# Sharing transposes two tiles at a time from tile 2 on, a later first output product, and a modulation vector folded by DMA, in an adaLN block with linear attention and a token mixer

## The chip, the cores and the metric

The kernel runs on one core of a Trainium2 chip. A core has TensorE (matrix products, "PE" in the profile), VectorE (DVE), ScalarE (ACT), GpSimd (POOL) and SyncE (SP, which here only issues transfers). The metric is the time of one execution on the device in microseconds, less being better; a kernel's time is the median of its runs.

## The reference

One token sequence x of 2048 x 448 goes through an attention half and a token-mixing MLP half. Both are modulated by six vectors of 448 that come from one condition vector c:

```python
mod = (silu(c) @ w_mod).reshape(1, 6, 1, -1)
sa, ca, ga, sb, cb, gb = (mod[:, j] for j in range(6))
h = layernorm(x) * (1 + ca) + sa
x = x + ga * A(h)          # linear attention
h = layernorm(x) * (1 + cb) + sb
x = x + gb * B(h)          # token-mixing MLP

# A: 16 heads of 28; phi(t) = where(t > 0, t + 1, exp(t)) + 1e-6
q, k, v = split(h @ wqkv)
kv = einsum("bhsd,bhse->bhde", phi(k), v);  z = sum over s of phi(k)
o = (phi(q) @ kv) / (phi(q) . z + 1e-6)
A = o @ wo
# B: the MLP runs over the token axis, F = 1792
u = gelu(einsum("bsd,sf->bdf", h, w1) + b1)
B = transpose(einsum("bdf,fs->bds", u, w2) + b2)
```

All data are float32.

## The kernel before

The 2048 tokens lie in 16 tiles of 128 rows by 448 channels (NT = 16). A float32 product is made of three TensorE products of a reduced float32 type: each operand is cut into a high part (a rounding copy, on ScalarE) and a low part (the difference, on VectorE), and high x high, high x low and low x high are added up in one PSUM bank. Channels are taken in chunks of 128; the fourth chunk has only 64 channels, and the other 64 rows of it can hold something else, such as low parts. That is how a product of 448 channels takes eleven matmuls instead of twelve: the 64 remaining channels of the high part and of the low part lie in one 128-row operand.

The order in which each engine works is written out by hand, in the order of the code; each engine works through its own list, and a step waits only for the data and the buffers that it needs. So what stands ahead of a step on its engine delays it, also where the two have nothing to do with each other.

The change lies in one stage, the loop `for i in range(NT + LAG)` with LAG = 5, from about 115 to 226 us. It runs the output side of the attention, the second layer norm, and the first GEMM of the MLP as a pipeline over tiles, and TensorE does in iteration i:

- the transposes of tile i (`b_transpose`, bank `tq`): the normalised q of the tile, `pn`, is turned chunk by chunk so that channels lie on partitions;
- output product i-1 (`b_out`, bank `op`): the transposed tile, in parts `pth` and `ptl`, times weights that hold wo with the attention state folded in. These weights are computed ahead of the loop in four groups of 112 rows (four heads each), in parts `wph` and `wpl`, and are moved by transfers into chunks of 128 rows, `oh` (high) and `ol` (low). Tile 0 uses the groups of 112, in twelve matmuls; the others use the chunks, in eleven;
- some q products of later tiles (`a_q`, bank `qp`, eleven matmuls each), as `QS` says: one an iteration, and two in iterations 0 and 4;
- from iteration 5 on, the step of w1's GEMM for tile i-5 (`step`, banks `up`).

VectorE and ScalarE do for the same tiles: the cut into `pth` and `ptl` (`b_high`, `b_low`); the residual `x` with its row sum (`b_res`, tile i-2); the second layer norm with its modulation in pieces (`b_norm1_a`, `b_norm1_b` on tile i-3, `b_norm2` on tile i-4), whose squares `sqa` (of x) and `sqb` (of y) are made on ScalarE and whose inverse roots `rt` and bias `nb` are made on GpSimd; the parts `h2h` and `h2l` of the result; and the normalisation of q for a tile ahead, s (`b_prod`, `b_sum`, `b_eps`, `b_recip`, `b_scale`: names `pd`, `den`, `pn`). `s` is i + 1, and i + 2 behind iteration LEAD = 4, in which two tiles are normalised. Between these, pieces of w1 are cut into `ph` and `pl` (`split_to`): the high and low part on ScalarE (L283, L284), and a transfer on GpSimd that adds (L285).

From tile B_PAIR = 6 on, tiles go in pairs: the fourth transpose of the first tile of a pair holds the last 64 channels of both tiles, the second tile has only three transposes, and two small transfers on SyncE (L850) bring the low parts where the product needs them. For tiles ahead of the pairs, VectorE copies the last 64 channels of `pn` next to themselves (`b_dup`), and each tile has four transposes.

Modulation vector 5 (gb) is also made in this stage. `w_mod`'s block lies as four tiles `wm` of 112 rows; `mod_part(5, k)` adds up the four, each scaled by its part of silu(c), in `acc` (the first on ScalarE, the others on VectorE). `mod_split` cuts `acc` into `mh` and `ml`, and `mod_sum2(5)`, at the start of iteration 16 and ahead of its `up` matmuls, adds their 112 rows with a matrix of ones into bank `modp`. For the vectors 2, 3 and 4 (`FOLDED`) rows 64 to 111 of `acc` are first added to rows 0 to 47 by an accumulating transfer on GpSimd (`fold`, L197), so that high and low part, 64 rows each, make one operand `mb` and one matmul:

```python
    def fold(j):
        nc.gpsimd.dma_start(macc[j][:G - 64], macc[j][64:], accum_op=ALU.add)

    def mod_split(j):
        acc = macc.pop(j)
        if j in FOLDED:
            macc[j] = moving(slot, f"mb{j}")
            split(acc[:64], macc[j][:64], macc[j][64:])
            return
```

(G is 112.) In the orders shown below, a number behind a name is the tile's, and the one behind the underscore the buffer's.

## Time and profile before

| | |
|---|---|
| median of 3 runs | 437.97 us (437.65 to 438.12) |
| the profiled execution | 438.2 us, of which the span from the first to the last instruction is 436.4 us |
| TensorE busy | 431.4 us (99% of the span) |
| VectorE busy | 365.6 us (84%) |
| ScalarE busy | 270.8 us (62%) |
| GpSimd busy | 122.1 us (28%) |
| granted TensorE clock | 1.000 |

"Busy" is the time in which an engine has an instruction in work; matmuls overlap in TensorE's pipeline, so the distance between the starts of two of them, and not the duration of one, is what one costs. In the profile's rows stand the start in us, the duration in us, the engine, the line of the kernel, the operation, the operands as out<-in, and in square brackets the idle time ahead of it and what ended that. The chain that ended last is followed back from the last instruction: at each step to what released it, or to the instruction before it on its engine.

### The profile page before, as it was taken

How to read it: one execution, taken by the hardware profiler on the slowest of the kernel's cores; microseconds unless marked ns; L12 is line 12 of the kernel's file. 1: busy time of each engine (PE TensorE's matmuls, PEld its weight loads, DVE VectorE, ACT ScalarE, POOL GpSimd, SP SyncE). 2: the span in 40 equal slices, each digit the busy share in tenths (PEclk: the TensorE clock that was granted, in tenths of full speed). 3: DMA queues.
4: the chain of work that ended last, by engine and by line, in shares of the span. 5: the costliest groups of instructions: out<-in, count | busy, mean ns of one | idle time of the engine just before them, and what ended most of it. 6: DMA issues, size and time to landing. Idle time of an engine off the chain costs nothing.

```text
span 436.4 us, 7337 instructions
## 1 busy us (share of the span) xinstructions
PE 431.4 (99%) x2390; PEld 401.8 (92%) x2390; DVE 365.6 (84%) x791; ACT 270.8 (62%) x581; POOL 122.1 (28%) x201
## 2 busy tenths in 40 slices
PE   8999999999999999999999999999999999999997
PEld 7699999999999999999999999999999999999996
DVE  5997898999899999985479487349999998898894
ACT  3768877765758787776766254235675555655650
POOL 2205767431034665554300000010112230230310
PEclk9999999999999999999999999999999999999999
DMA  8987999994442232524427456477667977977531
GB/s 223 307 220 117 175 206 237 223 226 140 139 124 50 39 65 58 145 66 90 127 84 237 166 161 183 125 183 196 153 141 188 187 161 181 183 162 202 88 43 44
DMA packets 66558, 65.97 MB, mean 151 GB/s; under 512 B 8776, under 2 KB 58072, under 8 KB 66520
## 3 DMA queue, kind: packets, MB, share of 16 engines
q1 hardware_dynamic: 55728, 48.41, 37.7%
q0 software_dynamic: 10784, 17.09, 24.9%
q8 instruction: 19, 0.31, 0.3%
q14 instruction: 19, 0.16, 0.1%
q10 hardware_dynamic: 8, 0.00, 0.0%
HBM read 41.88 MB, written 7.34 MB: 113 GB/s over the span
## 4 chain that ended last, share of the span: by engine, by line
PE 97%; DMA 1%; DVE 1%; SPq 0%; issue 0%; DVEq 0%
PE y L1129 19%; PE up L914 10%; PE up L916 10%; PE up L915 10%; PE y L1130 9%; PE op L864 8%; PE cacc L483 8%; PE qp L384 8%; PE kp L384 7%; PE tp L353 2%; PE tq L829 1%; DMA wm<-in_w_mod_dram 1%; PE kvb L757 1%; PE kp L532 1%; PE qp L532 1%; PE wp L934 1%
## 5 line engine op out<-in xcount | busy, mean ns | idle before, releaser
L914 PE MATMUL up<-h2h,ph 128*128 128x448 f32 x224 | 81.4, 363 | 0.0
L916 PE MATMUL up<-h2h,pl 128*128 128x448 f32 x224 | 81.3, 363 | 0.0
L915 PE MATMUL up<-h2l,ph 128*128 128x448 f32 x224 | 80.8, 361 | 0.0
L1089 POOL DMA_DIRECT2D a<-a x16 | 14.1, 969 | 147.2 <-PE up L915 75.6
L916 PEld LDWEIGHTS up<-h2h,pl 128*128 128x128 f32 x224 | 42.0, 188 | 3.2
L915 PEld LDWEIGHTS up<-h2l,ph 128*128 128x128 f32 x224 | 42.0, 187 | 2.8
L914 PEld LDWEIGHTS up<-h2h,ph 128*128 128x128 f32 x224 | 42.0, 188 | 2.4
L85 DVE TENSOR_TENSOR pl<-pr,ph 128x512 fp32r<-128x512 f32 x38 | 25.9, 689 | 11.4 <-ACT ph L84 8.8
L84 ACT ACTIVATE ph<-pr 128x512 fp32r<-128x512 f32 x38 | 23.2, 621 | 17.8 <-PE up L915 7.3
L1151 ACT ACTIVATE cc<-y 128x448 f32<-128x448 f32 x24 | 13.0, 544 | 22.8 <-PE y L1130 22.8
L483 PE MATMUL cacc<-pkh,xh 128*128 128x448 f32 x64 | 24.3, 379 | 0.0
L483 PE MATMUL cacc<-pkl,xh 128*128 128x448 f32 x64 | 23.2, 362 | 0.0
L1172 POOL DMA_DIRECT2D out_dram<-yt x14 | 13.2, 939 | 32.5 <-DVE yt L1158 23.0
L384 PE MATMUL qp<-wh,hh 128*128 128x448 f32 x60 | 21.6, 365 | 0.0
L384 PE MATMUL qp<-wh,hl 128*128 128x448 f32 x60 | 21.5, 363 | 0.0
L905 ACT ACTIVATE y<-y,nb,rt 128x448 f32<-128x448 f32 x16 | 12.2, 762 | 13.8 <-POOL nb L904 13.8
L384 PE MATMUL kp<-wh,hl 128*128 128x448 f32 x56 | 20.4, 364 | 0.0
L384 PE MATMUL kp<-wh,hh 128*128 128x448 f32 x56 | 20.3, 362 | 0.0
L330 POOL TENSOR_TENSOR rs<-ve,mhalf 128x1 f32<-128x1 f32 x16 | 13.7, 857 | 21.6 <-DVE ve L328 20.6
L864 PE MATMUL op<-oh,pth 128*128 128x448 f32 x50 | 19.4, 387 | 0.0
L1095 DVE TENSOR_TENSOR a<-a,s 128x512 f32<-128x512 f32 (+1 forms) x32 | 18.5, 621 | 0.0
L1129 PE MATMUL y<-ut,s1h 128*128 128x448 f32 x56 | 18.2, 376 | 0.0
(253 smaller groups left out, 1373.9 us busy)
## 6 DMA issues: line engine op xcount, KB each, us to landing
pr<-in_B_w_dram SPq DMA_DIRECT2D x56, 256.0 KB, 3.0
a<-in_B_w_dram SPq DMA_DIRECT2D x32, 256.0 KB, 4.2
a<-in_B_w_dram SPq DMA_DIRECT2D x32, 192.0 KB, 4.7
wm<-in_w_mod_dram SPq DMA_DIRECT2D x24, 196.0 KB, 4.8
x<-in_A_x_dram SPq DMA_DIRECT2D x16, 224.0 KB, 3.7
out_dram<-x SPq DMA_DIRECT2D x14, 224.0 KB, 2.0
out_dram<-yt POOLq DMA_DIRECT2D x14, 224.0 KB, 4.9
pk<-pk POOLq DMA_DIRECT2D x12, 224.0 KB, 4.3
```

What stands on the lines that cost most here:

```text
L84: nc.scalar.activation(hi, full, AF.Copy)
L85: nc.vector.tensor_sub(lo, full, hi.bitcast(F32))
L384: nc.tensor.matmul(o, a[:, ch * P:(ch + 1) * P], b, start=(n == 0), stop=(n == 10))
L483: nc.tensor.matmul(cacc[ch][:, :D], a[:, s], b, start=(t == 0 and i == 0), stop=(t == NT - 1 and i == len(todo) - 1))
L864: nc.tensor.matmul(opb[t][:, :D], a[:, g * P:(g + 1) * P], b, start=(n == 0), stop=(n == len(todo) - 1))
L914: nc.tensor.matmul(ps[:, :D], hi[:, sl], mh, start=first, stop=False)
L915: nc.tensor.matmul(ps[:, :D], hi[:, sl], ml, start=False, stop=False)
L916: nc.tensor.matmul(ps[:, :D], lo[:, sl], mh, start=False, stop=last)
L1089: nc.gpsimd.dma_start(w, a, accum_op=ALU.add)
L1095: nc.vector.tensor_tensor(w, raw2[q, a][i], raw2[q, b][i], op=op)
L1129: nc.tensor.matmul(ps[:, :D], h[:, s], w, start=opens and r == r0, stop=False, skip_group_check=True)
L1130: nc.tensor.matmul(ps[:, :HD], l[:, s], wh, start=False, stop=closes and r == PAIRS - 1 - (LAST if (q, m) == (NP - 1, 6) else 0), skip_gro ...
```

## The change

Four things, in the same loop:

- Pairs begin with tile 2 instead of 6 (`B_PAIR`), so (2,3) and (4,5) also share a fourth transpose. `LEAD` becomes 1: two tiles of q are normalised in iteration 1 instead of 4. The extra q product of iteration 4 moves to iteration 1 (`QS`).
- In iteration 1 the two q products come ahead of output product 0, which stands behind four q products altogether. It now uses the 128-row chunks `oh` and `ol`, in eleven matmuls, and so tile 0 is transposed with 128 columns a time and its last 64 channels are copied, like any other tile's.
- Vector 5 is folded like 2, 3 and 4: one `modp` matmul instead of two.
- The sums of vector 5 move: they were at the starts of iterations 13, 14 and 15 and at the end of 15; now two are at the end of iteration 13, two at the end of 14, with the fold behind them, and the split stays at the end of 15.

```diff
--- before.py
+++ after.py
@@ -34,12 +34,12 @@
 LAST = 3
 PRE2 = {16: (1, 0), 12: (1, 1), 8: (1, 2), 3: (4, 3), 1: (4, 4)}
 MOD_AT = {11: [(4, 0)], 12: [(4, 1)], 13: [(4, 2)], 14: [(4, 3)], 15: [(3, 0), (3, 1)]}
-QS = {0: 2, 4: 2}
-B_PAIR = 6
-LEAD = 4
+QS = {0: 2, 1: 2}
+B_PAIR = 2
+LEAD = 1
 REM = 3 * P
 SPLIT_AT = (8, 8, 9, 10, 11, 12, 12, 13, 13, 14, 14, 15, 15, 16, 17, 18)
-FOLDED = (2, 3, 4)
+FOLDED = (2, 3, 4, 5)
 WARM = 9
 ACT_STATS = ()
 PRE = 9
@@ -773,6 +773,7 @@
     b_prod(1)
     b_recip(0)
     b_scale(0)
+    nc.vector.tensor_copy(pns[0][:, D:], pns[0][:, REM:D])
     mod_out(4, mp)
     a_phi_q()
     b_sum(1)
@@ -822,14 +823,14 @@
     def b_transpose(t):
         pn = pns[t]
         tps[t] = bank(f"tq{t}")
-        n = P if t else G
+        n = P
         pair, second = b_pair(t)
         for g in range(3 if second else 4):
             a = pns[t + 1] if pair and g == 3 else pn
             nc.tensor.transpose(tps[t][:n, g * P:(g + 1) * P], a[:, g * n:(g + 1) * n], ident)
 
     def b_high(t):
-        n = P if t else G
+        n = P
         pair, second = b_pair(t)
         if not second:
             phs[t] = (slot(f"pth{t}", 512, F32R, parts=n), slot(f"ptl{t}", 512, F32R, parts=n))
@@ -840,7 +841,7 @@
             nc.scalar.activation(phs[t + 1][0][:64, REM:], tps[t][:64, REM:], AF.Copy)
 
     def b_low(t):
-        n = P if t else G
+        n = P
         pair, second = b_pair(t)
         w = REM if second else 4 * P
         hi, lo = phs[t]
@@ -854,9 +855,7 @@
         opb[t] = bank(f"op{t}")
         todo = []
         for g in range(4):
-            if t == 0:
-                todo += [(ph, g, Wph[g]), (ph, g, Wpl[g]), (pl, g, Wph[g])]
-            elif g == 3 and b_pair(t)[0]:
+            if g == 3 and b_pair(t)[0]:
                 todo += [(ph, g, Wr[0]), (ph, g, Wr[64])]
             else:
                 todo += [(ph, g, Wp_hi[g]), (pl, g, Wp_hi[g])] + ([(ph, g, Wp_lo[g])] if g < 3 else [])
@@ -947,15 +946,17 @@
     for i in range(NT + LAG):
         if i == NT - 4:
             load_mod(5)
-        if NT - 3 <= i < NT:
-            mod_part(5, i - NT + 3)
         if i < NT:
             b_transpose(i)
+        nq = min(len(late), QS.get(i, 1))
+        if i == 1:
+            for _ in range(nq):
+                a_q(late.pop(0))
         if 0 <= i - 1 < NT:
             b_out(i - 1)
-        nq = min(len(late), QS.get(i, 1))
-        for _ in range(nq):
-            a_q(late.pop(0))
+        if i != 1:
+            for _ in range(nq):
+                a_q(late.pop(0))
         t = i - LAG
         mp = mod_sum2(5) if i == NT else None
         if t >= 0:
@@ -1003,18 +1004,25 @@
             b_low2(i - 4)
         if i == LEAD:
             wp_rest()
-            for f in (b_prod, b_sum, b_eps, b_recip, b_scale, b_dup):
+            for f in (b_prod, b_sum, b_eps):
                 f(s + 1)
         while lagging:
             phi_q_sum(lagging.pop(0))
+        if i == LEAD:
+            for f in (b_recip, b_scale, b_dup):
+                f(s + 1)
         a_phi_q(nq, lagging)
         if i == 0:
             split_low(8)
         load_to(14 + (i + 1) // 2)
         if res or norm1:
             b_rstd(i, 0 if res else 1, 2 if norm1 else 1)
+        if i in (NT - 3, NT - 2):
+            for k in (0, 1):
+                mod_part(5, 2 * (i - NT + 3) + k)
+        if i == NT - 2:
+            fold(5)
         if i == NT - 1:
-            mod_part(5, 3)
             mod_split(5)
         split_to(SPLIT_AT[i] if i < NT else 10 + (i + 1) // 2)
 
```

Lines behind the first inserted one (L776 of the changed kernel) are numbered one higher than before up to the output product, and one lower from there on: the residual is L872 for L873, the second normalisation's y is L904 for L905, `nb` L903 for L904.

VectorE, from the low part of tile 1's transposes to the residual of tile 0 and what follows it, before:

```order
224 L847 TENSOR_TENSOR ptl1_1713<-tq1_1682,pth1_1712 128x512
225 L700 RECIPROCAL den2_1717<-den2_1717 128x16
226 L704 SCALAR_TENSOR_TENSOR pn2_1722<-pq2_866,den2_1717 128x448
227 L820 COPY pn2_1722<-pn2_1722 128x64
228 L408 SCALAR_TENSOR_TENSOR pq7_1725<-eq7_1676,rq7_1677 128x448
229 L873 SCALAR_TENSOR_TENSOR x0_91,sm0_1767<-op0_1687,x0_91 128x448
230 L690 SCALAR_TENSOR_TENSOR pd3_1769<-pq3_526,zb_1538 128x448
231 L694 TENSOR_REDUCE den3_1776<-pd3_1769 128x16
232 L847 TENSOR_TENSOR ptl2_1765<-tq2_1735,pth2_1764 128x512
```

and in the changed kernel:

```order
225 L848 TENSOR_TENSOR ptl1_1725<-tq1_1683,pth1_1724 128x512
226 L700 RECIPROCAL den2_1729<-den2_1729 128x16
227 L704 SCALAR_TENSOR_TENSOR pn2_1734<-pq2_866,den2_1729 128x448
228 L690 SCALAR_TENSOR_TENSOR pd3_1742<-pq3_526,zb_1538 128x448
229 L694 TENSOR_REDUCE den3_1744<-pd3_1742 128x16
230 L408 SCALAR_TENSOR_TENSOR pq7_1747<-eq7_1677,rq7_1678 128x448
231 L700 RECIPROCAL den3_1744<-den3_1744 128x16
232 L704 SCALAR_TENSOR_TENSOR pn3_1750<-pq3_526,den3_1744 128x448
233 L821 COPY pn3_1750<-pn2_1734 128x64
234 L872 SCALAR_TENSOR_TENSOR x0_91,sm0_1796<-op0_1712,x0_91 128x448
235 L690 SCALAR_TENSOR_TENSOR pd4_1798<-pq4_620,zb_1538 128x448
236 L694 TENSOR_REDUCE den4_1805<-pd4_1798 128x16
```

The whole normalisation of tile 3 (pd, den, reciprocal, pn) now stands ahead of the residual x0, and behind x0 comes tile 4's instead of tile 3's; the copy for the shared transpose takes tile 2's channels into tile 3's buffer.

ScalarE, around the end of iteration 13, before:

```order
266 L313 ACTIVATE sqb9_2589,vs12_2574<-y9_2577,ny9_2587 128x448
267 L184 ACTIVATE acc5_2599<-wm5_0_2519,sc_158 112x448
268 L837 ACTIVATE pth13_2559<-tq13_2601 128x384
269 L905 ACTIVATE y9_2577<-y9_2577,nb9_2634,rt12_2597 128x448
270 L908 ACTIVATE h2h9_2637<-y9_2577 128x448
271 L313 ACTIVATE sqa11_2643,vs13_2642<-x11_863,nm11_2640 128x448
272 L313 ACTIVATE sqb10_2655,vs13_2642<-y10_2645,ny10_2653 128x448
273 L283 ACTIVATE ph15_2668<-pr15_1531 128x512
274 L284 ACTIVATE pl15_2669<-ph15_2668 128x512
275 L837 ACTIVATE pth14_2703<-tq14_2674 128x512
```

and in the changed kernel:

```order
270 L904 ACTIVATE y9_2579<-y9_2579,nb9_2634,rt12_2599 128x448
271 L907 ACTIVATE h2h9_2637<-y9_2579 128x448
272 L313 ACTIVATE sqa11_2643,vs13_2642<-x11_863,nm11_2640 128x448
273 L313 ACTIVATE sqb10_2655,vs13_2642<-y10_2645,ny10_2653 128x448
274 L184 ACTIVATE acc5_2668<-wm5_0_2521,sc_158 112x448
275 L283 ACTIVATE ph15_2671<-pr15_1531 128x512
276 L284 ACTIVATE pl15_2672<-ph15_2671 128x512
277 L838 ACTIVATE pth14_2705<-tq14_2676 128x512
```

The first sum of vector 5 (L184) stood ahead of the high part of tile 13's transposes; it now stands one iteration later, between the squares and the two pieces of w1.

GpSimd, end of iteration 14, in the changed kernel:

```order
150 L896 TENSOR_SCALAR vw14_2736<-vs14_2721 128x2
151 L898 TENSOR_TENSOR rt14_2738<-vw14_2736,mhalf_87 128x2
152 L197 DMA acc5_2668<-acc5_2668 48x448
153 L285 DMA pl16_2744<-pr16_1533 128x512
154 L903 TENSOR_TENSOR nb11_2779<-ny11_2731,rt14_2738 128x1
```

Before, the piece's transfer (L285) stood right behind `rt14`; now the fold (L197) stands between them, ahead of `nb11`, for which ScalarE's y11 waits.

## The prediction

> **What bounds the kernel now.** I read the page first (busy shares, clock, chain), then the waits of TensorE, then the chain and the timelines of the stage that changes.
>
> ```profile
> span 436.4 us, 7337 instructions
> ...
> PE 431.4 (99%) x2390; PEld 401.8 (92%) x2390; DVE 365.6 (84%) x791; ACT 270.8 (62%) x581; POOL 122.1 (28%) x201
> ...
> PEclk9999999999999999999999999999999999999999
> ...
> PE 97%; DMA 1%; DVE 1%; SPq 0%; issue 0%; DVEq 0%
> ```
>
> TensorE is busy for 431.4 of 436.4 us, the chain that ended last runs 97% over it, and its granted clock never drops. The list of TensorE's waits has two entries, the larger of them:
>
> ```profile
> PE warm L148 <- DVE mhalf L102: 1.1, 1, 1.1
> ```
>
> Both lie in the first microseconds. So in the changed stage (about 115 to 226 us) TensorE never waits: each matmul that goes saves its pitch, as long as nothing new makes TensorE wait. The question is therefore whether the operands still come in time. The chain in that stage:
>
> ```profile
> 120.55 0.44 PE tq L829 x4
> 120.99 2.40 PE op L864 x12
> ...
> 126.05 2.21 PE op L864 x11
> ...
> 194.65 0.33 PE tq L829 x3
> ```
>
> A 448-wide matmul takes 2.21/11 = 0.20 us of the chain, a transpose 0.44/4 = 0.11 us. The end of the stage that matters is modulation vector 5, on TensorE's timeline:
>
> ```profile
> 201.63 0.37 PE L214 MATMUL modp<-mh,ones_r 112*128 112x448 f32 x1
> 201.83 0.37 PE L215 MATMUL modp<-ml,ones_r 112*128 112x448 f32 x1
> 202.04 0.37 PE L914 MATMUL up<-h2h,ph 128*128 128x448 f32 x1
> ```
>
> **What is saved on TensorE.** Output product 0: twelve matmuls become eleven, 2.40 − 2.21 = 0.19 us, taken as 0.20. Pairs (2,3) and (4,5) share their fourth transpose: two transposes of 0.11, 0.22 us. Vector 5: two matmuls become one, 0.20 us. Sum 0.62 us, 0.14% of the time. The first tile's transposes write 128 rows instead of 112: same count, nothing. This is all that the change can gain. By 201.63 the first two items are in, so the matmul of vector 5 is reached at 201.63 − 0.42 = 201.21 if nothing waits.
>
> **What is moved early.** Output product 0 goes behind two more q products (22 matmuls, 4.4 us): it is issued at 120.99 + 4.42 = 125.41. It now needs the folded weights oh and ol, which the second output product at 126.05 already used without a wait; 0.64 us earlier I take as free, the bound being 0.64 if they came just then. The residual x0 of tile 0 is then later, and so is everything behind it on VectorE, in order:
>
> ```profile
> 124.39 0.62 DVE L873 SCALAR_TENSOR_TENSOR x<-op,x 128x448 f32<-128x448 f32 x1
> ...
> 124.93 0.62 DVE L690 SCALAR_TENSOR_TENSOR pd<-pq,zb 128x448 f32<-128x448 f32 x1
> 125.59 0.62 DVE L694 TENSOR_REDUCE den<-pd 128x16 f32<-128x448 f32 x1
> ...
> 127.33 0.24 DVE L700 RECIPROCAL den<-den 128x16 f32<-128x16 f32 x1
> 127.60 0.62 DVE L704 SCALAR_TENSOR_TENSOR pn<-pq,den 128x448 f32<-128x448 f32 x1
> ...
> 131.65 0.68 DVE L887 SCALAR_TENSOR_TENSOR y<-y,rt,mod 128x448 f32<-128x448 f32 x1
> ```
>
> Before, x0 stood at 124.39 and the second half of its normalisation, y0, at 131.65. Now op0 ends at 127.62, so x0 starts at 127.67. Between x0 and y0, VectorE also does a whole extra tile of q normalisation (pd, den, reciprocal, pn: by the starts above 0.6 + 0.6 + 0.3 + 0.6, some 2 us), since tile s+1 is prepared in iteration 1 instead of 4 and every later iteration is one tile ahead. Walking VectorE's new order with these durations gives y0 at 134.1, 2.46 us later. What waits for y0 is the loop between ScalarE and GpSimd that makes the second normalisation:
>
> ```profile
> 137.39 0.76 ACT L905 ACTIVATE y<-y,nb,rt 128x448 f32<-128x448 f32 x1 [1.00 <-POOL nb L904]
> ...
> 186.41 0.76 ACT L905 ACTIVATE y<-y,nb,rt 128x448 f32<-128x448 f32 x1 [0.90 <-POOL nb L904]
> ...
> 187.69 0.66 ACT L313 ACTIVATE sqa<-x,nm 128x448 f32<-128x448 f32 x1
> ...
> 188.35 0.66 ACT L313 ACTIVATE sqb<-y,ny 128x448 f32<-128x448 f32 x1
> ...
> 189.00 0.62 ACT L283 ACTIVATE ph<-pr 128x512 fp32r<-128x512 f32 x1
> 189.65 0.64 ACT L284 ACTIVATE pl<-ph 128x512 fp32r<-128x512 f32 x1
> ...
> 190.67 0.25 ACT L840 ACTIVATE pth<-tq 64x128 fp32r<-64x128 f32 x1
> ...
> 191.90 0.76 ACT L905 ACTIVATE y<-y,nb,rt 128x448 f32<-128x448 f32 x1 [0.98 <-POOL nb L904]
> ```
>
> ```profile
> 189.18 0.34 POOL L897 TENSOR_SCALAR vw<-vs 128x2 f32<-128x2 f32 x1 [1.59 <-ACT sqb L313]
> 189.60 0.72 POOL L899 TENSOR_TENSOR rt<-vw,mhalf 128x2 f32<-128x2 f32 x1
> 190.69 0.95 POOL L285 DMA_DIRECT2D pl<-pr  x1 [0.37 <-ACT pl L284]
> 191.38 0.49 POOL L904 TENSOR_TENSOR nb<-ny,rt 128x1 f32<-128x1 f32 x1
> ```
>
> Each y waits for GpSimd's nb, nb for rt, rt for ScalarE's squares, and those follow the y before: a ring that keeps its own time. From tile 0's y at 137.39 to tile 10's at 191.90 there are ten turns, 54.5 us, 5.45 each; where y is late it stays late unless ScalarE had idle time to give. Iteration 4 has one q product fewer now, and its two ScalarE steps come from here:
>
> ```profile
> 133.46 0.52 ACT L402 ACTIVATE eq<-qp 128x448 f32<-128x448 f32 x1
> 133.88 0.53 ACT L403 ACTIVATE rq<-qp 128x448 f32<-128x448 f32 x1
> ```
>
> They step 0.42 and 0.43, so 0.85 us comes back there; some 0.3 us more comes back in two turns where the second square had waited for something off the ring, and TensorE's own early iterations, which were not late, give back a part too. That leaves a lateness d of the ring of +0.5 to +1.1 us from tile 4 on; nothing excludes less, so the ends I keep are −0.4 (the ring goes with TensorE, which is 0.42 earlier) and +2.46 (nothing comes back). I take 0.7.
>
> **The added small things.** Per new pair, one ScalarE copy of 64 rows (0.25 us above) and two SyncE transfers of 32 KB, whose record is
>
> ```profile
> DMA to landing us min/median/max: 1.7/2.2/3.4
> ```
>
> against two duplicate copies on VectorE that go. The pair (4,5) needs its pieces for output product 4 about 4.2 us after the low half is cut: covered by the slowest of these ten. ScalarE and VectorE wait in those iterations (1.00 us for nb above), so nothing is added.
>
> **Vector 5, the step that decides.** Before, its sums and its split:
>
> ```profile
> 184.41 0.65 ACT L184 ACTIVATE acc<-wm,sc 112x448 f32<-112x448 f32 x1
> ...
> 200.01 0.58 ACT L84 ACTIVATE mh<-acc 112x448 fp32r<-112x448 f32 x1
> ```
>
> ```profile
> 194.94 0.72 POOL L899 TENSOR_TENSOR rt<-vw,mhalf 128x2 f32<-128x2 f32 x1
> 196.18 0.92 POOL L285 DMA_DIRECT2D pl<-pr  x1 [0.52 <-ACT pth L837]
> ...
> 200.63 0.63 DVE L85 TENSOR_TENSOR ml<-acc,mh 112x448 fp32r<-112x448 f32 x1 [0.65 <-ACT mh L84]
> ```
>
> The low half ends at 201.26 and its matmul starts at 201.83: 0.57 us of slack. The step on ScalarE at 184.41 stood where ScalarE then waited 0.90 for nb anyway; in the changed order it stands between the squares of iteration 13 and the two pieces ph and pl, and GpSimd's piece transfer waits for pl, nb waits behind that transfer, and y behind nb: +0.65 on the ring. In iteration 14 the accumulating transfer goes into GpSimd's queue ahead of the next piece transfer. Its issue holds GpSimd as long as the piece's does (190.69 to 191.38 in the rows of GpSimd above: 0.69 us), and GpSimd had waited 0.52 there: +0.17. Its own record:
>
> ```profile
> L197 POOL DMA_DIRECT2D acc<-acc x3: 809/815/1127, 67.3 to 99.0; - x3
> ...
> DMA to landing us min/median/max: 3.6/4.6/4.7
> ```
>
> It starts behind rt of iteration 14, at 194.94 + 0.72 + 0.65 + 0.1 = 196.4 + d, and lands at 200.0 to 201.1 + d. ScalarE is free for the split at 200.01 + 0.82 = 200.83 + d. So the high half starts at 200.83 to 201.1 + d, takes 0.56 to its reader, the low half 0.04 and 0.62 more: ready at 202.05 to 202.35 + d. One matmul holds both halves, so it waits for the low one: TensorE, there at 201.21, stands 0.85 to 1.15 us + d. The up matmul behind it starts 0.20 later, with a tenth for the hand-over at most: 202.30 to 202.65 + d instead of 202.04. All that TensorE saved before is swallowed in this wait; the sum is +0.26 to +0.6 + d, and with d = 0.7 it is +1.0 us. Behind vector 5 the next up products need pieces and tiles that stand 0.6 us or more ahead, so I take that nothing is added there. VectorE queues the residual of tile 14 behind the low half; that tile's up product comes some 20 us later.
>
> The Trainium skill ("DMA: Bandwidth & Descriptors", section "Anatomy of one DMA — SWDGE (gpsimd) path") gives 2.0 us and bytes/436e3 for a transfer that GpSimd issues. For the 86 KB here that is an estimate of 2.2 us; the rows of 3.6 to 4.7 say more, and I go by them. By the page the fold would be there before ScalarE is free, and the sum would be 0.3 + d, at the low end of mine.
>
> **Rivals.** *The fold is in time* (the other side): the ring is not later than before and the transfer lands near 3.6, and the small delays of 0.65 and 0.17 fall into waits. It decides if the low half is ready by 201.21, so about 1 us earlier than I have it with d = 0. Against it: slack before was 0.57, and a transfer of at least 3.6 us is put into a chain that had none. Then −0.62: 437.58 for the profiled execution's kind, 437.35 as median. *The ring keeps up with TensorE* (d from −0.4 to 0.3): vector 5 waits, yet only for what was added to it: −0.1 to +0.85, about 438.3. For it: the tile-10 y was reached with 0.98 of wait for nb, and TensorE's early iterations were not late. *An early wait decides instead*: the shared transposes of pairs need the tile after them, two iterations' worth of VectorE work sooner. Such a wait shifts TensorE, and only the part beyond the 1.5 us that vector 5 costs anyway would show; three of 0.5 us would be needed for a further +0.5: 439.5. *The clock falls*: a wait of 2 us at vector 5 might lower TensorE's clock behind it; half speed for as long as the wait lasted would add 1 us more, 440.0. No row speaks for it: the clock is 9 in every slice, with the 1.1 us wait near the start among them.
>
> The Trainium skill ("TensorE: Matmul & The Clock Gate", section "What's actually happening") has the clock halved after an idle window of about 3.4 us; by that rule a wait of 1.5 to 2 us leaves it alone, which is why I give that rival little.
>
> **How the numbers follow.** The sum is against the profiled execution's 438.2 us (span 436.4 and 1.8 around it), which is 0.23 above the median of 437.97. 438.2 + 1.0 = 439.2, and less 0.23 the median becomes 439.0. This kernel's runs differ by 0.47 us, so 0.2% (0.88 us: 437.09 to 438.85) is about what can be told from no change. Chances: a wait at vector 5 with d of 0.5 or more, 0.52; the ring keeps up, 0.30; fold in time, 0.12; early waits 0.04; clock 0.02. Slower by over 0.2% holds most of the first, early waits and clock: 0.52. Same holds the ring, the fold and the rest of the first: 0.43. Faster would need more than the 0.62 us there are to gain: 0.05 for the scatter. The range reaches down to the fold in time, 437.3, and up to d = 1.9, 440.2.
>
> **What would show it.** TensorE's waits list one entry, the single matmul of vector 5 behind the low half on VectorE, of 1.2 to 2.2 us. The first y on ScalarE stands near 139.9 (137.39 before), tile 10's, with the 0.65 on the ring, 1.2 to 1.8 later than its 191.90. Output product 0 starts near 125.4 with no wait. I am wrong if that entry is missing, if the ring is not later than before by tile 10, or if TensorE waits earlier, at the transposes of tile 4, 6 or 8 or at product 4.

## The result: 3.9 us slower, and the profile after

The changed kernel takes 441.82 us (441.41 to 442.3, four runs), the kernel before 437.93 beside it: a ratio of 1.0089 (95% interval 1.0076 to 1.0102). The forecast was slower, 439.0; the time lies outside its range of 437.3 to 440.2. The profiled execution took 442.3 us with a span of 439.8.

The page of the changed kernel, first its span, busy shares, clock and chain:

```profile
span 439.8 us, 7342 instructions
...
PE 433.2 (98%) x2386; PEld 402.9 (92%) x2386; DVE 365.5 (83%) x790; ACT 269.9 (61%) x583; POOL 120.0 (27%) x202
...
PEclk9999999999999999998999999999999999999999
...
PE 92%; ACT 4%; POOL 2%; DVE 1%; issue 1%; ACTq 0%; DVEq 0%; POOLq 0%
```

TensorE has four matmuls fewer and is busy for 1.8 us more. One slice of the clock shows an 8, and the chain now runs 6% over ScalarE and GpSimd, where it had none. TensorE's waits (in all, times, longest):

```profile
PE modp L211 <- DVE mb L85: 1.8, 1, 1.8
PE warm L148 <- DVE mhalf L102: 1.1, 1, 1.1
PE op L863 <- ACT rq L403: 0.4, 1, 0.4
```

The first and the last are new. (`warm` lies in the first microseconds, before and after.) TensorE's timeline at vector 5, and a window (busy times of the engines, clock, DMA) behind it:

```profile
203.37 0.47 PE L211 MATMUL modp<-mb,ones_r 128*128 128x448 f32 x1 [1.82 <-DVE mb L85]
203.68 0.36 PE L913 MATMUL up<-h2h,ph 128*128 128x448 f32 x1
...
204.46 0.57 PE L913 MATMUL up<-h2h,ph 128*128 128x448 f32 x1
204.83 0.57 PE L914 MATMUL up<-h2l,ph 128*128 128x448 f32 x1
...
207.07 0.56 PE L914 MATMUL up<-h2l,ph 128*128 128x448 f32 x1
207.44 0.39 PE L915 MATMUL up<-h2h,pl 128*128 128x448 f32 x1
207.67 0.37 PE L913 MATMUL up<-h2h,ph 128*128 128x448 f32 x1
```

```profile
203.40:207.60 4.20, 4.20 (x13) 3.77 (x14) 2.59 (x7) 3.08 (x7) 1.55 (x4) 0.59 0.36 62
```

Behind the wait of 1.82 us the matmuls start 0.37 us apart instead of 0.20, from 204.1 to 207.5, and the granted clock of that window is 0.59: TensorE ran at half speed for 3.4 us. Matmuls matched between the two traces give the account: the first transposes of the stage are 0.48 earlier than before (the start-up of this one execution), the last matmul of output product 15 is 0.25 earlier, the first up matmul behind vector 5 is 1.64 later, and behind the slow stretch all are 3.23 later. So up to product 15 the change loses 0.24, vector 5 costs 1.88, the slow stretch 1.59: 3.7 us in all. The two profiled executions differ by 4.1 us (442.3 and 438.2), their spans by 3.4.

What the forecast called the ring, y on ScalarE of tiles 0, 10 and 11:

```profile
139.58 0.76 ACT L904 ACTIVATE y<-y,nb,rt 128x448 f32<-128x448 f32 x1 [1.42 <-POOL nb L903]
...
193.30 0.76 ACT L904 ACTIVATE y<-y,nb,rt 128x448 f32<-128x448 f32 x1 [0.98 <-POOL nb L903]
...
199.52 0.76 ACT L904 ACTIVATE y<-y,nb,rt 128x448 f32<-128x448 f32 x1 [1.98 <-POOL nb L903]
```

In the kernel before they stood at 137.39, 191.90 and 197.36. In what follows, "late" is against the kernel before with both traces laid on the stage's first transposes: 2.67 at y0, 1.08 at y4, 1.32 at y9, 1.88 at y10, 2.64 at y11.

### The profile page after: what moved, and what is told of

The parts are those of the page before. It is cut to its first block, busy times and chain, and to the rows that moved or that the text cites. A ratio compares the mean times of both kernels' runs of the same rounds, so it can differ in the third digit from the quotient of the medians.

```text
span 439.8 us, 7342 instructions
## 1 busy us (share of the span) xinstructions
PE 433.2 (98%) x2386; PEld 402.9 (92%) x2386; DVE 365.5 (83%) x790; ACT 269.9 (61%) x583; POOL 120.0 (27%) x202
## 4 chain that ended last, share of the span: by engine, by line
PE 92%; ACT 4%; POOL 2%; DVE 1%; issue 1%; ACTq 0%; DVEq 0%; POOLq 0%
PE y L1137 19%; PE up L915 10%; PE up L914 10%; PE up L913 10%; PE y L1138 9%; PE cacc L483 8%; PE kp L384 7%; PE qp L384 6%; PE op L863 6%; PE tp L353 1%; PE warm L148 1%; POOL pl L285 1%; PE tq L830 1%; PE kvb L757 1%; ACT y L904 1%; PE qp L532 1%
## 5 line engine op out<-in xcount | busy, mean ns | idle before, releaser
L914 PE MATMUL up<-h2l,ph 128*128 128x448 f32 x224 | 81.8, 365 | 0.0
L904 ACT ACTIVATE y<-y,nb,rt 128x448 f32<-128x448 f32 x16 | 12.2, 763 | 19.8 <-POOL nb L903 19.8
L1054 DVE TENSOR_TENSOR u<-u,mod 128x448 f32<-128x448 f32 x14 | 8.7, 621 | 12.3 <-ACT u L1053 12.1
```

Source lines behind the costliest of these rows:

```text
L904: nc.scalar.activation(ys[t], ys[t], AF.Identity, bias=nb, scale=rs)
L914: nc.tensor.matmul(ps[:, :D], hi[:, sl], ml, start=False, stop=False)
```

## The experiments

In all runs the kernel before was timed on the same chip beside them: 437.9 to 438.1 us. Theory 1: TensorE's end of this stage is set by the ring, which is late in part from the early tiles and in part from vector 5's steps, and the long wait then lowers the clock. The rivals stand with each run; runs are called e1 to e15.

**The wait put elsewhere (e1).** In iteration 16:

```diff
-        mp = mod_sum2(5) if i == NT else None
+        mp = None
...
             step(t, accs, H2h[t], H2l[t], t == 0, t == NT - 1)
+        if i == NT:
+            mp = mod_sum2(5)
```

> The changed kernel with the one matmul of vector 5 issued behind the up matmuls of tile 11 instead of ahead of them (2.4 us later on TensorE, later than its operand is ready). Theory 1, the ring between ScalarE and GpSimd is late, and vector 5 is only the first place where TensorE meets it: the wait moves to the next place, the bank of output product 15 that the fourth bank of w1's second group needs (its residual stands behind the low part of tile 12 on VectorE, near 208.0 us, TensorE there at 205.8): about 2.2 us of wait, and the time stays within 0.5 us of the changed kernel, 441.3 to 441.8. Rival, only vector 5's own sums and fold are late: the wait goes, nothing follows, and the time is 437.97 - 0.62 saved + 0.43 of the wait at product 5, near 438.0, with the clock at 1.000.

442.01 us, ratio 1.0089 (1.0072 to 1.0107). TensorE's waits:

```profile
PE up L913 <- DVE x L872: 2.0, 1, 2.0
```

The wait moved whole to the fourth bank of tile 11's up matmuls, as theory 1 has it. In three of six runs the mean clock was 0.996, in the others, the profiled one among them, 1.000; their spans were 440.3 to 440.7 and 438.6 to 439.6.

**The two halves of the change.** First vector 5 alone, in the kernel before (e2):

```diff
-FOLDED = (2, 3, 4)
+FOLDED = (2, 3, 4, 5)
...
+        if i in (NT - 3, NT - 2):
+            for k in (0, 1):
+                mod_part(5, 2 * (i - NT + 3) + k)
+        if i == NT - 2:
+            fold(5)
```

(the old calls of `mod_part(5, ...)` removed)

> The kernel before with part 3 and 4 of the change alone: vector 5 folded, its sums at the ends of iterations 13 and 14. The ring is late by only what these add near its end (0.65 for the sum on ScalarE and about 0.75 for the fold's issue on GpSimd, as the profile of the changed kernel has them). Theory 1: the low half is ready near 202.6 and TensorE, there at 201.63, waits about 1.0 us: 438.6 to 438.9, no fall of the clock, since the wait is half of that in the changed kernel. Rival, vector 5 alone makes the whole of the loss: near 441.

439.56 us, 1.0035 (1.0023 to 1.0047). Then the rest of the change without it (e3):

```diff
-FOLDED = (2, 3, 4, 5)
+FOLDED = (2, 3, 4)
```

(and the sums of vector 5 back in their old places, without `fold(5)`)

> The changed kernel with vector 5 as before (two matmuls, sums at the starts of iterations 13 to 15, no fold); pairs from tile 2, LEAD 1 and the late product 0 stay. Theory 1: the ring is late by about 0.6 to 1.0 us to its end, TensorE waits 0.4 at product 5, and again 0.4 to 0.8 at the low half of vector 5 or behind it; 0.42 is saved: 438.3 to 439.0, clock 1.000. Rival, the early part is harmless (all of it vector 5's): 437.97 - 0.42 + 0.43, near 438.0.

439.42 us, 1.0033 (1.0022 to 1.0045). The waits, of vector 5 alone and of the rest alone:

```profile
PE modp L211 <- DVE mb L85: 0.7, 1, 0.7
```

```profile
PE op L863 <- ACT rq L403: 0.4, 1, 0.4
PE modp L215 <- DVE ml L85: 0.2, 1, 0.2
```

Vector 5 alone: y late by 0.00 up to tile 9, 0.56 at tile 10, 1.32 at tile 11. The rest alone: 2.67 at tile 0, 1.28 from tile 9 on. The two add up to 2.60, close to the 2.64 of the changed kernel at y11. Both cost 0.4 to 0.7 us more than expected: a wait costs more than its listed length, since the first matmul behind it starts 0.3 ahead of the next, and both meet a second, shorter wait at the fourth bank (0.2 to 0.3 us by the matched matmuls at 206). 1.6 and 1.4 make 3.0, and 0.9 of the changed kernel's loss is left. By the matched matmuls TensorE ends the first GEMM 1.12 (e2) and 1.14 (e3) late; with both halves it is 2.44 where the clock held (e1 and e4, below) and 3.71 in the changed kernel's trace. So only 0.2 of the rest is a wait; the others are the slow stretch, where it comes, and time outside the span (at the end of the next section).

**The clock (e4, e7, e9).** Nine matmuls into the bank of vector 5, ahead of its own:

```diff
         ps = bank(f"modp{j}")
+        if j == 5:
+            for _ in range(9):
+                nc.tensor.matmul(ps[:, :D], ones_r, Wp_hi[0], start=True, stop=True)
```

> The changed kernel with nine matmuls more, whose result is overwritten, ahead of vector 5's: TensorE is busy for 1.8 us of the wait, and its operand comes no sooner. If the fall of the clock behind the wait comes from TensorE's idleness: the clock is 1.000 in every run and the profile has no matmuls of 0.37 us pitch behind vector 5; the time falls by what the slow matmuls cost in the profile, 11 x 0.17 = 1.9 us, in those runs that had it: 440.0 to 441.0. Rival, the clock falls for another reason (load or time of the run): the same clocks and time as the changed kernel, 441.8.

440.85 us, 1.0069 (1.0056 to 1.0082), the clock 0.998 to 1.000 in five runs. On TensorE:

```profile
201.58 1.99 PE L212 MATMUL modp<-oh,ones_r 128*128 128x448 f32 x9
203.57 0.47 PE L214 MATMUL modp<-mb,ones_r 128*128 128x448 f32 x1
203.88 0.37 PE L916 MATMUL up<-h2h,ph 128*128 128x448 f32 x1
204.09 0.36 PE L917 MATMUL up<-h2l,ph 128*128 128x448 f32 x1
```

Work that serves nothing, put into the wait, takes 1 us off the median of the changed kernel: the operand comes no sooner, but the matmuls behind it keep their 0.20. The clock held five times of five, where half of the runs of the changed kernel and of e1 had lost it; by luck alone that would be 1 in 32. TensorE ends 2.44 late instead of 3.71, so the slow stretch costs 1.3 us net: 0.3 of its 1.6 would have gone to a wait at the fourth bank. To see how long a wait lowers the clock, vector 5's matmul went behind two of the four groups of tile 11, which splits the wait:

```diff
...
+                for f, ps in enumerate(accs):
+                    acc3(ps, hi, lo, slice(f * P, (f + 1) * P), H2h[t], H2l[t], False, False)
+                    if f == 1:
+                        mp = mod_sum2(5)
```

> The changed kernel with vector 5's matmul behind two of the four groups of tile 11's up matmuls, 1.2 us later. Theory 1: the 2.2 us that TensorE has to wait for the ring split into about 0.7 at vector 5 and 1.2 to 1.5 at the fourth bank, the place of TensorE behind both is that of the run with the matmul behind all four groups. The clock tells how long a wait lowers it: if waits up to 1.5 us leave it alone, 1.000 in every run and 440.6 to 441.2; if what counts is the sum of idleness over a few us, 0.996 in half of the runs as in the changed kernel, 441.5 to 442.5.

440.78 us, 1.0072 (1.0060 to 1.0084); 0.999 or 1.000 in five runs, with waits of

```profile
PE up L913 <- DVE x L872: 1.3, 1, 1.3
...
PE modp L211 <- DVE mb L85: 0.5, 1, 0.5
```

And ahead of output product 15 instead of behind it (`mod_sum2(5)` moved above `b_out(i - 1)`):

> The changed kernel with vector 5's matmul ahead of output product 15 instead of behind it: TensorE reaches it 2.2 us earlier, so it waits 1.8 + 2.2 = 4.0 us in one piece, and the product and all behind it come 2.2 us later than in the changed kernel. If a longer idle stretch lowers the clock more surely: 0.996 or lower in every run (2 of 4 in the changed kernel), and 441.5 + 2.2 + 0.9 to 1.7 = 444.5 to 445.5. Rival, the fall has nothing to do with the wait's length: 0.996 in about half of the runs, and some runs at 443.5.

444.94 us, 1.0164 (1.0145 to 1.0182); the clock 0.992 once and 0.996 three times, in four runs:

```profile
PE modp L211 <- DVE mb L85: 4.1, 1, 4.1
```

A stretch of 3.4 us at half speed takes 0.004 off a run's mean clock, so 0.996 is one such stretch and 0.992 are two. (The 0.998 that some runs show is not one: in e15's profiled execution it comes from the last 1.4 us, behind the last matmul.) Each kernel's wait is known from its one profiled execution. Where the longest in this stage is 0.7 to 1.3 us, no run has such a stretch (e2, e5, e7, e8, e11, e13, e14, e15: 52 runs); where it is 1.8 to 2.0, five of ten have one (the changed kernel and e1); where it is 4.1, four of four.

What divides the runs of one kernel can be read from the clock that the traces record. Within a trace it changes only in steps of 3.41 us (the changed kernel: 58 steps at full speed, one at half, 68 at full), and where these steps lie differs from execution to execution. The step that holds the wait and the one behind it, in the changed kernel and then in e1's profiled execution, which kept its clock (behind the ends and the length of the step stands TensorE's busy time; the third number from the end is the granted clock):

```profile
200.66:204.07 3.41, 1.59 (x8) 1.17 (x7) 1.97 (x5) 3.35 (x9) 0.92 (x2) 1.00 0.18 31
204.07:207.48 3.41, 3.41 (x11) 3.01 (x11) 1.80 (x5) 2.32 (x6) 1.55 (x4) 0.50 0.45 77
```

```profile
203.57:206.98 3.41, 2.51 (x13) 2.00 (x11) 1.80 (x6) 2.29 (x5) 1.56 (x4) 1.00 0.41 71
206.98:210.39 3.41, 2.29 (x11) 2.16 (x12) 2.37 (x6) 1.76 (x5) 1.99 (x5) 1.00 0.46 109
```

In the changed kernel all 1.82 us of the wait lie in one step, and the next step runs at half speed. In e1 the 2.0 us fall across a boundary, 0.90 in one step and 1.12 in the next, and nothing follows. The 4.1 us of e9 reach over two steps:

```profile
198.23:201.64 3.41, 1.80 (x9) 1.33 (x8) 1.44 (x5) 1.40 (x4) 2.35 (x5) 1.00 0.78 163
201.64:205.05 3.41, 0.90 (x5) 0.87 (x6) 2.24 (x5) 3.28 (x8) 1.02 (x3) 1.00 0.08 13
205.05:208.46 3.41, 3.41 (x11) 3.01 (x10) 1.75 (x5) 2.40 (x6) 1.45 (x4) 0.50 0.45 77
```

Behind the step with 1.6 us of idleness the clock is whole, behind the one with 2.5 it is half. So in these three traces the idle time inside one step tells whether the next runs at half speed, and what is needed lies between 1.6 and 1.8 us, about half a step; no run moved the steps on purpose to prove it. By this a wait of 1.8 to 2.0 us is caught or not by where the steps happen to lie: with 1.7 as what is needed, in some 0.54 to 0.59 of all executions, an estimate from these figures.

**Is it the ring (e5, e8, e6)?** The changed kernel with a shorter ring, the low halves of three pieces of w1 made by VectorE, off ScalarE and GpSimd:

```diff
-PIECE_DMA = tuple(range(8, 18))
+PIECE_DMA = tuple(range(8, 15))
```

> The changed kernel, but the low halves of w1's pieces 15, 16 and 17 are made by one subtraction on VectorE (which idles 1.9 us in each of these iterations) instead of a copy on ScalarE and an accumulating transfer on GpSimd, so that in iterations 13 to 15 nothing stands between rt and nb on GpSimd but the fold. Theory 1, what counts is when the ring between ScalarE and GpSimd ends: y of tile 10 and 11 come some 1 us earlier each, TensorE's wait at vector 5 falls from 1.8 to under 0.7 us and the wait of the fourth bank goes, clock 1.000 in every run: 438.0 to 438.8. Rival, the fold's landing or its place sets the wait: the wait stays above 1.3 us and the time above 440.5.

439.95 us, 1.0045 (1.0032 to 1.0058); TensorE's wait at vector 5 was 1.1. The clock held, but the wait fell only by 0.7: neither side's numbers. y10 came 1.4 earlier than in the changed kernel, y11 only 0.7 earlier. GpSimd and VectorE between them:

```profile
196.04 1.76 POOL L898 TENSOR_TENSOR rt<-vw,mhalf 128x2 f32<-128x2 f32 x1
```

```profile
195.22 1.40 DVE L188 SCALAR_TENSOR_TENSOR acc<-wm,sc,acc 112x448 f32<-112x448 f32 x2
196.54 0.68 DVE L85 TENSOR_TENSOR pl<-pr,ph 128x512 fp32r<-128x512 f32 x1
```

rt on 128 x 2 numbers took 1.76 us instead of 0.72 while VectorE did two sums, a subtraction and the residual behind it. With the matmul of vector 5 behind the up matmuls as well:

> Both: low halves of pieces 15 to 17 on VectorE, and vector 5's matmul behind tile 11's up matmuls. Theory 1: no wait over 0.3 us behind 200 us; left are the 0.43 us at output product 5, the 0.62 saved and some 0.2 of restart: 437.7 to 438.2, clock 1.000. Rival, the ring's lateness is met elsewhere in the up matmuls of tiles 12 and 13: 439 or more.

440.63 us, 1.0063 (1.0051 to 1.0076): missed, on the rival's side. The fourth bank waits 1.3 us, and ScalarE shows why:

```profile
204.74 0.55 ACT L166 ACTIVATE mod<-modp 128x448 f32<-128x448 f32 x1 [1.72 <-PE modp L211]
205.18 0.75 ACT L904 ACTIVATE y<-y,nb,rt 128x448 f32<-128x448 f32 x1
```

The copy of vector 5 out of its bank stands ahead of tile 12's y. Moving the matmul back kept ScalarE waiting 1.7 us, and what e5 had won at y12 was lost again.

The other test leaves out work: the kernel before without the products of the low part of tiles 6, 7 and 8 with the high weights (nine matmuls).

```diff
-                todo += [(ph, g, Wp_hi[g]), (pl, g, Wp_hi[g])] + ([(ph, g, Wp_lo[g])] if g < 3 else [])
+                todo += [(ph, g, Wp_hi[g])] + ([] if g < 3 and t in (6, 7, 8) else [(pl, g, Wp_hi[g])]) + ([(ph, g, Wp_lo[g])] if g < 3 else [])
```

> The kernel before with nine matmuls left out (the low part of the transposed tile times the high weights in output products 6, 7 and 8): 1.8 us less on TensorE, nothing moved elsewhere. Theory 1, the ring keeps its own time and stood only 0.4 to 0.6 us behind TensorE's needs in the kernel before: waits of 0.7 to 1.2 us in sum appear at vector 5 and behind it, and the time falls by 0.4 to 0.7 only: 437.3 to 437.6. Rival, the ring follows TensorE: no new wait, 438.0 - 1.8 = 436.2.

438.44 us, 1.0012 (1.0002 to 1.0021): 1.8 us less work gains nothing, which is neither side's number. The profile has the tile 10 and 11 rows of the ring at

```profile
191.59 0.76 ACT L905 ACTIVATE y<-y,nb,rt 128x448 f32<-128x448 f32 x1 [0.98 <-POOL nb L904]
197.04 0.76 ACT L905 ACTIVATE y<-y,nb,rt 128x448 f32<-128x448 f32 x1 [1.22 <-POOL nb L904]
```

which is 0.3 earlier than before, as are this execution's first transposes (0.32). All sixteen y's are 0.30 to 0.32 earlier, with no step at the tiles that cost TensorE less: the ring keeps its own time. But the ring takes only part of the gain. By the matched matmuls 1.1 of the 1.8 us was gone at 172 us, at two waits that are not for y: 0.2 for the transfer of a pair's low part and 0.4 for `pn` of the q normalisation, each costing more than its listed length; 0.6 more went at vector 5 and the fourth bank, where the ring is met, and TensorE left this stage 0.13 early. This execution then waits 1.5 us for VectorE at the second GEMM (`PE y` on `DVE ut`); the other runs' spans were shorter (435.9 to 437.3), and that wait is not followed further here.

**What makes the ring late early on (e12, e13).** The forecast put it on the late product 0 and the tile normalised ahead. From the run without the fold, product 0 as before (twelve matmuls, ahead of the q products):

> The run with the pairs only, with output product 0 as in the kernel before: twelve matmuls behind two q products, in iteration 1 ahead of the q products. Pairs from 2, LEAD 1 and the q products' numbers stay. It parts the two causes of the ring's early lateness (1.2 to 1.3 us at the end with the pairs only): product 0, 4.4 us later, or the tile normalised ahead of it on VectorE. If product 0: y0 is late by about 1.2 instead of 2.4 and y11 by 0.3 at most, no wait behind 200 us, 437.7 to 438.1. If the tile: as with the pairs only, 439.4.

439.76 us, 1.0040 (1.0027 to 1.0052); y0 late by 2.60, the end by 1.26: moving product 0 back alone gains nothing. That does not acquit it. VectorE's rows of the changed kernel and of e12:

```profile
127.14 0.62 DVE L872 SCALAR_TENSOR_TENSOR x<-op,x 128x448 f32<-128x448 f32 x1 [0.82 <-PE op L863]
```

```profile
129.10 0.69 DVE L847 TENSOR_TENSOR ptl<-tq,pth 128x512 fp32r<-128x512 f32 x1 [0.74 <-ACT pth L840]
```

In the changed kernel VectorE stands 0.82 us for product 0 ahead of x0, as the forecast had it. With the product in place it stands 0.74 a little later for the copy of tile 2's transposes, which follow the same two q products on TensorE: the one path stands behind the other. Then the q products too as before:

```diff
-QS = {0: 2, 1: 2}
+QS = {0: 2, 4: 2}
```

> The last run (pairs from 2, LEAD 1, product 0 as before) with the q products in the places of the kernel before (two in iterations 0 and 4). Left of the change: shared transposes and the tile normalised in iteration 1. If the q product moved into iteration 1 makes the ring late (it puts tile 2's transposes 2.2 us later, and ScalarE's square of x0 stands behind their copy in its queue): y0 at most 0.7 late, the ring's end at most 0.3, no new wait behind 200 us, 0.22 saved: 437.6 to 438.1. If the extra tile on VectorE does: y0 2.0 to 2.6 late and 1.0 or more left at the end: 439.2 to 439.8.

438.92 us, 1.0023 (1.0015 to 1.0032); y0 late by 1.12, the end by 0.53, between the two expectations. So of the 1.28 at the end the q product moved into iteration 1 makes 0.75. What is left, 0.5, comes with the tile normalised ahead, through VectorE's list or through a new wait of TensorE's (below); no run parts these two. ScalarE shows the way of the moved q product, in e12 and then in e13:

```profile
128.31 0.60 ACT L837 ACTIVATE pth<-tq 128x512 fp32r<-128x512 f32 x1 [4.92 <-PE tq L829]
...
128.96 0.66 ACT L313 ACTIVATE sqa<-x,nm 128x448 f32<-128x448 f32 x1
```

```profile
126.74 0.60 ACT L837 ACTIVATE pth<-tq 128x512 fp32r<-128x512 f32 x1 [3.65 <-PE tq L829]
...
127.52 0.67 ACT L313 ACTIVATE sqa<-x,nm 128x448 f32<-128x448 f32 x1
```

The square of x0 (`sqa`) stands behind the copy of tile 2's transposes (`pth`), and these behind the q products on TensorE. In e13 no wait is left behind 200 us; its loss is a new one at 126:

```profile
PE tq L829 <- DVE pn L820: 0.7, 1, 0.7
```

the shared fourth transpose of tile 2, which needs tile 3's pn; with two q products ahead of it the change had hidden that.

**Fold or sums (e14).** The changed kernel with vector 5's sums at the starts of iterations 11 to 14:

> The changed kernel with vector 5's four sums at the starts of iterations 11 to 14 (its weights are loaded two iterations earlier); the fold stays where it is. It parts the fold's issue from the two sums that stood side by side on VectorE beside vw and rt. If the sums make the larger part (0.56 us at y10 and 0.45 of the 0.76 at y11): y10 no later than y9, y11 0.3 to 0.5 more, the wait at vector 5 from 1.8 to 0.8 to 1.1, clock 1.000: 440.0 to 440.6. If the fold's issue does: y11 0.7 or more later than y10, the wait above 1.2, 440.7 or more.

440.6 us, 1.0063 (1.0050 to 1.0077); the wait at vector 5 is 0.9, the clock 1.000 five times. y10 is 0.09 later than y9 (0.56 in the changed kernel), y11 0.59 later than y10 (0.76). So the sum on ScalarE cost 0.5, the fold's issue on GpSimd 0.6, the two sums beside vw and rt 0.2. In their new places the sums still cost something: y9 is 1.50 late instead of 1.32, so the move gains 0.47 at y11.

**Can it be had without loss (e10, e11, e15)?** The pairs without the fold, with the shorter ring:

> Pairs from tile 2, LEAD 1 and the late product 0 with vector 5 as before (the run with the pairs only), and the low halves of w1's pieces 15 to 17 made on VectorE. No fold and no pair of sums stands beside rt and nb now. Theory 1, the loss is the ring's lateness at its end: y of tile 10, 11 and 12 come 0.8 us or more earlier each than with the pairs only, no wait at vector 5 or at the fourth bank, 0.43 at product 5 stays: 437.7 to 438.3. Rival, something else of the pairs costs the time: 439.2 to 439.6 as with the pairs only.

438.4 us, 1.0010 (1.0001 to 1.0019). No wait is left in the stage but the one at product 5, and y10 and y11 come 0.15 and 0.75 earlier than in the kernel before:

```profile
PE op L863 <- ACT rq L403: 0.4, 1, 0.4
```

So 0.9 us of the 1.4 that the pairs cost alone goes with the ring's lateness. One q product more moved forward (two in iteration 2) to take away that last wait:

> The same with one q product more moved forward (two in iteration 2, none in the last). If the wait at output product 5 comes from the last q product's exponentials on ScalarE, which hold its bank: that wait goes too, and with 0.42 saved on TensorE the time is 437.4 to 437.8, just below the kernel before. Rival, the early part of the ring gets later by the moved product (two ScalarE steps of 0.43 more ahead of y0) and waits come back: 438.0 to 439.0.

439.84 us, 1.0045 (1.0032 to 1.0058), the rival's side and beyond it: y0 is late by 3.95, TensorE waits 0.8 at the transposes of tile 8 for pn. And the pairs with product 0 and q products as before and the shorter ring:

> Pairs from 2 with product 0 and q products as before, vector 5 as before, and the low halves of pieces 15 to 17 on VectorE. If no wait is left: 0.22 saved on TensorE and nothing lost, 437.6 to 437.9, level with the kernel before within what can be measured. If TensorE meets another late engine: 438.3 or more.

438.89 us, 1.0019 (1.0010 to 1.0028): the 0.7 at tile 2's transposes stays. No version beats the kernel before.

## Why the prediction was right in direction and wrong in size

The steps that failed: in the sum for vector 5 the lateness of the ring (d, 0.7 taken, 1.28 measured) and the fold's issue (0.17 taken, 0.76 measured) were too small, so the operand came 0.75 to 1.05 us later than taken; and behind vector 5, where the sum puts nothing, up to 0.3 us of wait or 1.6 us of slow matmuls followed. Term by term:

- The bound: right. TensorE waited for nothing before, and the loss comes through new waits and what follows them.
- The savings of 0.62: right as a count, with nothing left of them. Before product 15 0.42 is saved and 0.66 lost again, through a wait at output product 5 that the forecast did not have: its bank is held by the last q product, whose exponentials on ScalarE stand behind the late ring. An early wait was a rival with a chance of 0.04, looked for at the transposes of tiles 4, 6 or 8 or at product 4. As that rival says, it adds nothing of its own while vector 5 waits: the operand of vector 5 comes when it comes, and without the early wait TensorE would have stood there so much longer.
- Product 0 behind four q products: the matmuls ran without a wait, as said. Laid on the kernel before, x0 started at 127.62 (127.67 forecast), and y0 came at 139.58 (139.9 forecast), 2.67 late (2.46 forecast). What the forecast's walk along VectorE did not have is the second path of the same length: e12 gives 2.60 with the product in place. With the q products back too (e13) 1.12 is left, so the moved q product, which holds up product 0 and tile 2's transposes alike, and the extra tile on VectorE make y0 late.
- The lateness d: 0.7 taken, 1.28 measured (e3), beyond the upper end of 0.5 to 1.1 though within the outer bounds. The forecast's 2.46 less its two credits of 0.85 and 0.3 is 1.31, close to what was measured; the further "part" given back by TensorE's own early iterations was not there.
- The sum on ScalarE: +0.65 forecast, 0.56 measured. The fold's issue: +0.17 forecast, 0.76 measured at y11, of which e14 leaves 0.59 to the fold. This is, with d, the term that was mis-sized most. The forecast let the issue fall into the 0.52 us that GpSimd had waited ahead of the next piece's transfer. The rows of the changed kernel:

```profile
196.06 0.64 POOL L896 TENSOR_SCALAR vw<-vs 128x2 f32<-128x2 f32 x1 [2.42 <-ACT sqb L313]
196.78 0.72 POOL L898 TENSOR_TENSOR rt<-vw,mhalf 128x2 f32<-128x2 f32 x1
197.46 0.88 POOL L197 DMA_DIRECT2D acc<-acc  x1
198.09 1.18 POOL L285 DMA_DIRECT2D pl<-pr  x1
198.70 0.79 POOL L903 TENSOR_TENSOR nb<-ny,rt 128x1 f32<-128x1 f32 x1
```

vw took 0.64 instead of 0.19, beside the two sums on VectorE, so that rt ended (197.50) when ScalarE had already made pl (197.16), and hardly any wait was left to fall into; and nb behind two transfers in a row took 0.79 instead of 0.48.

- The fold's landing did not count: it landed 2.7 us after its issue, near 200.2 (3.6 to 4.7 was taken), and the split started on ScalarE only when that was free,

```profile
202.10 0.56 ACT L84 ACTIVATE mb<-acc 64x448 fp32r<-64x448 f32 x1
```

right behind the second square.
- The wait at vector 5: 1.55 to 1.85 by the forecast's terms, 1.82 measured. That is luck: ring and TensorE were both later. What counts is when the operand is ready: laid on the kernel before, 203.8 where the forecast's terms give 202.75 to 203.05. The three terms above (0.58 for d, -0.09 for the sum, 0.59 for the fold) make 1.08, all of that. Behind the wait TensorE is 2.12 late, where the forecast took 1.0.
- "Nothing is added behind vector 5": wrong. The fourth bank of w1's second group is 0.2 to 0.3 us late behind vector 5 (e2, e3, e4), and 1.3 to 2.0 as soon as vector 5 does not take the wait (e1, e7).
- The rival of the clock, chance 0.02 and price 1.0: it came, in two of four runs, at 1.6 us in the trace and 1.3 net of the wait that it took the place of. Without it the changed kernel still took 441.4 and 441.6 (its two runs with the clock at 0.999 and 1.000), and 440.85 with the wait filled: over the range for the other reasons alone. The wait of 1.1 us that the forecast held against this rival could not speak: it lies in the first 1.1 us, ahead of the first entry of that trace's clock record at 4.8. The Trainium skill ("TensorE: Matmul & The Clock Gate", section "What's actually happening") names an idle window of about 3.4 us as what halves the clock. Read as a wait of that length, as the forecast did, the runs contradict it: waits of 1.8 to 2.0 us were enough five times in ten. That the slow stretch lasted 3.4 us, and that the steps of the clock lie elsewhere in each execution, fits the page's sentence that the window is free-running; the idle time that was enough inside one window lies, by the traces above, between 1.6 and 1.8 us.

Left open: the span and the time differ by 1.7 to 1.8 us in the kernel before and by 2.0 to 2.8 in the four runs of the changed one. Nothing in the traces shows why; some 0.2 to 1.0 us of its loss lies there.

## What to carry to other kernels

Where one engine is busy for 99% and never waits, ask how late the others may be before it does: here a ring over two other engines was 0.4 to 0.5 us from being the bound at vector 5 (y11 1.32 and 1.28 late in e2 and e3, TensorE 0.80 and 0.86), and two other steps were close as well, so 1.8 us of matmuls taken away gained nothing (e6), and what was put on the ring beyond that was paid. A saving of 0.6 us on the full engine is worth its count only if each step that it moves stays off that ring, and a wait is followed to the next operand that has no slack before it is moved. A wait of about 2 us on TensorE cost another 1.3 us behind it in half of the runs; matmuls that serve nothing (e4), or splitting the wait (e7), kept the clock.

## What the runs showed of the hardware that I had not expected

TensorE's clock fell to half for 3.4 us behind a single wait of 1.8 to 2.0 us, in five of ten runs; with waits up to 1.3 us never in 52. It changes in steps of 3.41 us, and it fell behind a step with 1.8 us of idleness, not behind one with 1.6; a wait that fell across two steps, 0.9 and 1.1 us, left it alone. Small GpSimd instructions were longer beside VectorE's sums: vw 0.64 us instead of 0.19, rt 1.76 instead of 0.72. In these rows VectorE was at work on instructions with two inputs in SBUF (`acc<-wm,sc,acc`, `pl<-pr,ph`), and for the last 0.6 us of rt on the residual, which reads a bank of PSUM. The Trainium skill ("GPSIMD Engine Reference", section "8. Key points") says that GpSimd shares its SBUF interfaces with VectorE and contends with such instructions; the rows agree but for that end of rt. With the sums elsewhere (e14) vw still took 0.46, so the sums make only part of it.
